# A tuned attention and feed-forward kernel whose written order is planned anew: sixteen planning passes, loads assumed at their full listed time, the first value load moved to GpSimd's queue

## The chip, the cores and the metric

One core of a Trainium2 chip runs the whole program. TensorE (PE) multiplies, and its weight loads are shown as PEld; VectorE (DVE), ScalarE (ACT) and GpSimd (POOL) work between the products; SyncE (SP) issues nearly all transfers. The metric is the device time of one execution in microseconds (us), smaller is better.

## The reference, cut to what matters

```python
def _attn_ref(q, k, v):                      # (4, 12, 448, 64) each
    scores = scale * np.matmul(q, k.transpose(0, 1, 3, 2)) - np.log(S)
    attn = 1.0 / (1.0 + np.exp(-scores))     # sigmoid, no sum over a row
    return np.matmul(attn, v)
def _moe_ref(x, w1, w2, w3, w_out):          # x: (1792, 768)
    h = np.maximum(np.maximum(x @ w1, x @ w2), x @ w3)
    return h @ w_out
def _moe2_ref(x, w_gate, w_val, w_out):      # d_ff 1536
    g = x @ w_gate
    return (g / (1.0 + np.exp(-g)) * (x @ w_val)) @ w_out
```

The output of attention, its heads side by side, goes through `_moe_ref` and the result through `_moe2_ref`. Everything is float32.

## The kernel before, in words

Every float32 factor of a dense product is split into a high and a low part, and three products of parts make one of the whole. The 1792 tokens are worked in two sets: set 0 holds the first 768 tokens, set 1 the other 1024.

**Stages on TensorE.** Attention runs in 12 quads (a quad is two pairs of heads of one batch), each of seven score groups: three of the first pair (`ps<-qq,kk`, six matmuls each), one that serves both (`ps<-qT,kT`), three of the second. ScalarE turns each group into `a` by one sigmoid (`a<-ps`), and later matmuls multiply `a` with the values (`av<-a,rv`). Two `ps` buffers exist, so that score group n+2 needs the sigmoid of group n. Once the first batches are through, products of the first dense layer of set 0 (`m<-x,w`, 18 matmuls each, 36 such products) stand between the groups. Then come the second layer of set 0, both layers of set 1 (by a scheme of seven products in place of eight), the gated layer for both sets (factors named `T` for set 1, `Z` for set 0) and the output product.

**Loads.** A pair needs four transfers each for `rq` and `rk` (56 KB each) and a quad three for `rv`. VectorE transposes `rq` and `rk` to `qT` and `kT`, and ScalarE, VectorE or GpSimd split these into `qq` and `kk`. A dense weight comes as `wraw` (768 KB, two buffers); ScalarE rewrites its words in two steps (`r<-wraw`, L483 and L496) and VectorE in two more (`c`), since the words must be put into the range of the parts; then it is split into `w`, and `c` is stored (`dp<-c`) for set 1.

**Who sets the order.** No engine chooses at run time. The program writes down tasks with their possible engines, an assumed duration and a due time; `Plan.order` runs through them once with a model of engines, queue and buffers, always starts the task that can start first (within a small slack the one with the earliest due time) and so fixes engine and place of every instruction. An instruction that waits holds everything behind it on its engine. A transfer on SP is assumed to take `SPF` = 0.88 of its listed time in a common queue, plus `TAIL` = 1800 ns, and SP's issue of one to take `ISSUE` = 530 ns. Due times come from TensorE's planned order and are passed back once over the tasks (`due_times`).

Of the kernel before, what the change touches and what calls it, by code (L numbers as in the profile page):

```python
# [1 line left out]

# [55 lines left out]
SPF = 0.88  # L58
# [12 lines left out]
NEAR = 6  # L71
AHEAD0 = 170.0 * 1000.0
# [6 lines left out]
ISSUE = 530.0  # L79
# [4 lines left out]
BACK = 3  # L84
# [7 lines left out]
class Plan:  # L92
# [9 lines left out]
    def __init__(self):  # L102
        self.tasks = []
        self.kind = None

    def add(self, opts, fn, reads=(), writes=(), after=(), due=math.inf, tail=0.0, port=False, wait=(), early=0.0, issues=1, late=0.0):
        deps = {id(w): w for w in (*after, *wait) if w is not None}
        deps.update((id(w), w) for b in (*reads, *writes) for w in b.writers)
        data = {id(w) for b in (*reads, *writes) for w in b.writers} | {id(w) for w in wait}
        new = [b.root for b in writes if b.root.ring is not None]  # L110
        deps.update((id(b.ring.opener), b.ring.opener) for b in new if b.ring.opener is not None)
        load = opts.get("sp", 0.0) * SPF
        if load:
            opts = {"sp": ISSUE * issues}
        t = Task(opts, fn, list(deps.values()), new, due, tail, port)
        t.data, t.early, t.load, t.late, t.issues = data, early, load, late, issues
        t.kind = self.kind
        for b in writes:
            b.writers.append(t)
        for b in (*reads, *writes):  # L120
            b.root.users.append(t)
        self.tasks.append(t)
        return t

    def due_times(self):
        for t in reversed(self.tasks):
            t.due = t.aim
            d = LEAD.get(t.kind, 0.0) + max(min(t.opts.values()), t.load)
            for s in t.succ:
                lat = (0.0 if "pe" in t.opts and "pe" in s.opts else self.LAT) + (t.tail if id(t) in s.data else 0.0)  # L130
                t.due = min(t.due, s.due - d - lat)

# [6 lines left out]
    def order(self):  # L139
# [40 lines left out]
        while open_:  # L180
# [13 lines left out]
            first = min(x[0] for x in best[e])  # L194
# [22 lines left out]

    def run(self, engines):
        for t in self.tasks:
            for d in t.deps:  # L220
                d.succ.append(t)
        self.due_times()
        length, done = self.order()
        for t, e, at in done:
# [4 lines left out]
        return length  # L229
# [27 lines left out]
def sigmoid_attention_max_ffn_silu_ffn(tc, q, k, v, w1, w2, w3, wo, wg, wv, wo2, out):  # L257
# [505 lines left out]
    def load_pair(b, h0):  # L763
# [15 lines left out]
        for src, r in ((q, rq), (k, rk)):  # L779
# [35 lines left out]
        fetch(rv, 2200.0, load_v, 3, "pairv" if b or h0 else "pair")  # L815
        return rq, rk, rv

    half_p = [slice(0, D), slice(D, P)]
# [531 lines left out]
    def gated(facs1, kept):  # L1350
# [5 lines left out]
        def factors(w, i):  # L1356
            plan.kind = "w"
            if i == 0:
                if id(w) in again:
                    left = left_again(again[id(w)])  # L1360
                    plan.kind = "b"
                    return left
                again[id(w)] = []
            left = seven(w, i, None if i else again[id(w)])
# [3 lines left out]
        ts = {}  # L1368
        for j, (w, use) in enumerate(((wg, silu(1, ts)), (wv, gate(1, ts, 0)))):
            left = factors(w, 0)  # L1370
            stream(1, left, facs[1], use)
            plan.kind = "x"
            facs[0].append(recall(j, kept[j]))
        rows, sums = EARLY_ROWS, 0
        for i in range(1, KG // 2):
            ts = {}
            for j, w in enumerate((wg, wv)):
                left = factors(w, i)
                for s in (1, 0):
                    stream(s, left, facs[s], gate(s, ts, i) if j else silu(s, ts))  # L1380
                    if len(facs[0]) < HD:
                        plan.kind = "x"
                        facs[0].append(recall(2, kept[2]))
                        plan.kind = "b"
                plan.kind = "w"
                if (i > 1 or j) and rows >= 2 * (sums + 1):
                    rows_sums(sums, due_p + 20000.0)
                    sums += 1
                if rows < KG:
                    rows_ahead(rows, due_p + 20000.0)  # L1390
                    rows += 1
                plan.kind = "b"
            if i == BACK:
                ts = {}
                for j, w in enumerate((wg, wv)):
                    stream(0, factors(w, 0), facs[0], gate(0, ts, 0) if j else silu(0, ts))
# [127 lines left out]

    plan.kind = "h"
    attention()
    turn([att, ps], [pmb, half, rest0])
    plan.kind = "w"
    for u in range(NU):
        weight(0, u)  # L1530
    todo = [(w, 2 * i + j) for i in range(KG // 2) for w in (wg, wv) for j in range(2)]
    for i, (w, f) in enumerate(todo[:NEAR]):
        ahead(w, f, False, AHEAD0 + (i + 1) * (AHEAD1 - AHEAD0) / NEAR, raw, AHEAD0 + i * (AHEAD1 - AHEAD0) / NEAR)
# [20 lines left out]
    for f in range(EARLY_ROWS):  # L1554
        rows_ahead(f, due_p)
    facs = second_layer(1, hs)
# [38 lines left out]
```

## Time and profile before

| what | value |
|---|---|
| median of 3 runs | 962.94 us (962.07 to 963.49) |
| profiled execution | 964.14 us, its span 962.0 us |
| instructions in the span | 13288 |
| TensorE busy | 942.6 us, 98% |
| VectorE, ScalarE, GpSimd busy | 667.5, 444.0, 92.1 us |
| mean granted TensorE clock | 0.990 |
| moved by DMA | 174.16 MB, 181 GB/s |

The span goes from the first to the last instruction; the execution's own time is 2.14 us longer. TensorE is nearly always busy, so time can change where it waits, where its clock is low, or where its work itself changes.

### The profile page before, as it was taken

What the parts mean: (1) busy time and instruction counts of PE and PEld (TensorE: products, weight loads), DVE (VectorE), ACT (ScalarE), POOL (GpSimd) and SP (SyncE); (2) the same over time, 40 slices, a digit from 0 to 9 for tenths busy, and PEclk for the clock granted to TensorE, in tenths of its full rate; (3) what the DMA queues carried; (4) which work ended last, traced back from release to release, by engine and by line L of the source; (5) the groups of instructions that cost most, each with busy time, mean ns of one, the idle gap of its engine ahead of it and who ended that gap; (6) DMA issues with size and microseconds to landing.
All of it is one profiled execution on the core that took longest, in us unless ns stands there. A gap on an engine that the chain in (4) does not pass through costs nothing.

```text
span 962.0 us, 13288 instructions
## 1 busy us (share of the span) xinstructions
PE 942.6 (98%) x4969; PEld 793.9 (83%) x4969; DVE 667.5 (69%) x1015; ACT 444.0 (46%) x620; POOL 92.1 (10%) x76
## 2 busy tenths in 40 slices
PE   8999989999999999999999999999999999999998
PEld 3444757877799888887888888888988989999998
DVE  5646565456568888998889965666456659998672
ACT  5657555466556545455665523233133325333330
POOL 0000000000010113221013201110010100000000
PEclk9998989999999999999999999999999999999999
DMA  7678878856569755556758474745844538621211
GB/s 115 130 142 191 222 197 213 243 187 203 189 194 324 238 187 180 179 172 197 256 187 278 148 224 140 225 164 171 282 141 138 169 106 326 230 83 50 99 58 66
DMA packets 196160, 174.16 MB, mean 181 GB/s; under 512 B 98304, under 2 KB 174592, under 8 KB 196096
## 3 DMA queue, kind: packets, MB, share of 16 engines
q1 hardware_dynamic: 192848, 172.91, 59.1%
q10 hardware_dynamic: 3248, 0.40, 0.3%
q8 instruction: 39, 0.64, 0.3%
q14 instruction: 25, 0.20, 0.1%
HBM read 115.74 MB, written 57.54 MB: 180 GB/s over the span
## 4 chain that ended last, share of the span: by engine, by line
PE 86%; DMA 5%; DVE 3%; SPq 2%; ACT 2%; issue 1%; DVEq 0%; ACTq 0%
PE m L1013 32%; PE av L1013 22%; PE mm L1013 22%; PE av L894 5%; PE ps L865 4%; DMA wraw<-in_moe_w_dram 2%; SPq L785 2%; DMA rk<-in_k_dram 1%; PE ps L858 1%; DMA rq<-in_q_dram 1%; DMA w<-dlS 1%; DVE S L622 1%; DMA dp<-S 1%; DVE Z L381 0%; DVE u L1193 0%
## 5 line engine op out<-in xcount | busy, mean ns | idle before, releaser
L1013 PE MATMUL mm<-T,w 128*128 128x512 f32 x567 | 138.0, 391 | 0.0
L1013 PEld LDWEIGHTS mm<-T,w 128*128 128x128 f32 x567 | 106.1, 188 | 21.6 <-DVE u L1193 0.4
L1013 PEld LDWEIGHTS m<-x,w 128*128 128x128 f32 x648 | 112.9, 190 | 11.4 <-issue 6.4
L1013 PE MATMUL m<-x,w 128*128 128x384 f32 x648 | 120.2, 341 | 0.0
L878 ACT ACTIVATE a<-ps,bias 128x896 f32<-128x896 f32 x84 | 80.8, 1003 | 42.9 <-PE ps L865 35.0
L1013 PE MATMUL m<-T,w 128*128 128x512 f32 x378 | 92.9, 390 | 0.0
L1013 PE MATMUL av<-T,w 128*128 128x512 f32 x378 | 92.5, 389 | 0.0
L1193 DVE TENSOR_TENSOR u<-mm,u 128x512 f32<-128x512 f32 (+1 forms) x93 | 59.0, 635 | 46.0 <-PE mm L1013 45.7
L1013 PEld LDWEIGHTS av<-T,w 128*128 128x128 f32 x378 | 71.0, 188 | 14.8
L1013 PEld LDWEIGHTS m<-T,w 128*128 128x128 f32 x378 | 70.8, 188 | 14.3
L865 PEld LDWEIGHTS ps<-qq,kk 64*128 64x128 f32 x432 | 45.9, 254 | 41.7 <-ACT a L878 28.6
L894 PE MATMUL av<-a,rv 128*64 128x448 f32 (+1 forms) x384 | 75.7, 564 | 0.1
L378 ACT CAST w<-G 128x768 fp32r<-128x768 f32 x47 | 39.4, 838 | 78.7 <-PE m L1013 33.7
L865 PE MATMUL ps<-qq,kk 64*128 64x448 f32 x432 | 62.6, 413 | 11.3 <-ACT a L878 10.2
L504 DVE SCALAR_TENSOR_TENSOR c<-c,r 128x768 int32<-128x768 int32 x48 | 51.1, 1064 | 31.9 <-ACT r L496 31.6
L483 ACT ACTIVATE r<-wraw 128x768 int32<-128x768 uint32 x48 | 43.7, 911 | 47.5 <-DMA wraw<-in_moe_w_dram 32.9
L1013 PE MATMUL mm<-Z,w 128*128 128x384 f32 x324 | 62.3, 336 | 0.0
L1013 PEld LDWEIGHTS mm<-Z,w 128*128 128x128 f32 x324 | 57.4, 188 | 1.9 <-DMA w<-dlS 0.2
L1013 PE MATMUL av<-wr,w 128*128 128x384 f32 x288 | 52.5, 334 | 0.0
L496 ACT ACTIVATE r<-wraw 128x768 f16<-128x768 f32 x48 | 52.0, 1084 | 0.5
L381 DVE TENSOR_TENSOR w<-G,w 128x768 fp32r<-128x768 f32 x49 | 46.6, 953 | 5.4 <-ACT w L378 5.4
L1013 PEld LDWEIGHTS av<-wr,w 128*128 128x128 f32 x288 | 50.1, 188 | 0.0
(141 smaller groups left out, 1482.7 us busy)
## 6 DMA issues: line engine op xcount, KB each, us to landing
cc<-dp SPq DMA_DIRECT2D x30, 768.0 KB, 5.1
dp<-c SPq DMA_DIRECT2D x48, 384.0 KB, 4.2
wraw<-in_moe_w_dram SPq DMA_DIRECT2D x18, 768.0 KB, 6.2
wraw<-in_moe_w_gate_dram SPq DMA_DIRECT2D x12, 768.0 KB, 4.9
wraw<-in_moe_w_val_dram SPq DMA_DIRECT2D x12, 768.0 KB, 5.1
cc<-in_moe_w_out_dram SPq DMA_DIRECT2D x12, 768.0 KB, 4.7
G<-dg SPq DMA_DIRECT2D x28, 320.0 KB, 7.0
rq<-in_q_dram SPq DMA_DIRECT2D x96, 56.0 KB, 2.6
```

The costliest lines, as they stand in the source:

```text
L378: (eng.copy if eng is nc.scalar else eng.tensor_copy)(o, i)
L381: eng.tensor_tensor(out=o, in0=a, in1=b, op=ALU.subtract)
L483: lambda e: e.activation(rb_at(), word(0).bitcast(U32), AF.Copy, scale=0.875 * 2.0 ** -29, bias=0.4999),
L496: lambda e: e.activation(rb_at().bitcast(F16).rearrange("p (c two) -> p c two", two=2)[:, :, 1], word(1).bitcast(F32), AF.Copy, scale=2.0 ...
L504: lambda e: e.scalar_tensor_tensor(c_at().bitcast(I32), c_at().bitcast(I32), 3, rb_at(), ALU.logical_shift_left, ALU.bitwise_or),
L622: return lambda e: e.tensor_tensor(out=o(), in0=x(), in1=y(), op=kind)
L785: eng.dma_start(out=r.t[D * j + 32 * e:D * j + 32 * e + 32], in_=src[b, h0 + j, :, 32 * e:32 * e + 32].rearrange("(c i) d -> i c d", i=32),)
L865: nc.tensor.matmul(psb.t[:, j, :S], kk.t[half_p[j], wh, cols], qq.t[half_p[j], xh], start=(i == 0), stop=(i == 2),)
L878: lambda e: e.activation(ab.t, psb.t[:, :, :S], AF.Sigmoid, bias=bias, scale=SCALE),
L894: nc.tensor.matmul(accs[g].t[half_p[j], :S], pairs[g][2].t[at, 2 * g + j, c], ab.t[at, j], start=first[g], stop=last[g],)
L1013: nc.tensor.matmul(acc.at(n), l(), r(), start=first and i == 0, stop=last and i == len(terms) - 1, skip_group_check=not (first and last),)
L1193: lambda e: e.tensor_tensor(out=o.t[:, :n], in0=acc.at(n), in1=x.t[:, :n], op=ALU.add),
```

## The change

Lines with `+` are new. The planner draws its plan sixteen times. After a pass, `again` takes the order that came out: due times of TensorE's tasks become the start times of a schedule without holes, tasks are ranked as placed, and a task that reuses a buffer hands its due time to the users of the buffer before it (`behind`). The pass with the smallest `cost` (holes in TensorE's planned order, plus `HALF` for each hole over 1600 ns) is kept; from the fourth pass on the due times of the best are shaken by up to 300 ns. On ScalarE and VectorE (`LOOK`) a task that is due sooner, and could start before the chosen one ends, goes first. Transfers are assumed to take 1.0 instead of 0.88 of their listed time up to the second layer of set 1 (`plan.full`), and 0.88 from there on; an issue 550 instead of 530 ns.

By hand, two loads move: the `rk` of the second pair, which ScalarE's queue issued, goes to SP's queue ahead of the same pair's `rq`, and the `rv` of the first quad goes from SP's queue to GpSimd's. The rewritten `gated` (not shown) puts down the same tasks as before with the values given: `BACK` was 3 already, so the first gated pair of set 0 stood in the middle of that stage before, too.

```diff
-SPF = 0.88
+SPF = 1.0
+SPF1 = 0.88
...
-ISSUE = 530.0
+ISSUE = 550.0
...
+LOOK = ("act", "dve")
+HALF = 2500.0
+TRIALS = 16
+SETTLE = 3
+SHAKE = 300.0
...
-        load = opts.get("sp", 0.0) * SPF
+        load = opts.get("sp", 0.0) * (SPF if self.full else SPF1)
...
-        for t in reversed(self.tasks):
+        for t in sorted(self.tasks, key=lambda t: t.rank, reverse=True):
...
+            for s in t.behind:
+                t.due = min(t.due, s.due - max(min(t.opts.values()), t.load) - (t.tail if "sp" in t.opts else 0.0) - self.LAT)
...
+            if e in LOOK:
+                soon = at + t.opts[e]
+                for x in best[e]:
+                    if at < x[0] < soon and x[1] < soon - SLACK and t.due > x[0] + x[2].opts[e] and x[1] < t.due:
+                        at, _, t = x
+                        soon = at
...
+    def cost(self, done):
+
+        last = total = 0.0
+        for at, t in sorted(((at, t) for t, e, at in done if e == "pe"), key=lambda x: x[0]):
+            total += max(0.0, at - last) + (HALF if at - last > 1600.0 else 0.0)
+            last = at + t.opts["pe"]
+        return total, last
...
+        for i in range(TRIALS):
+            if i >= SETTLE:
+                for t, state in best[3]:
+                    t.aim, t.rank, t.behind = state
+            self.due_times()
+            if i >= SETTLE:
+                for t in self.tasks:
+                    if "pe" not in t.opts:
+                        t.due += chance.uniform(-SHAKE, SHAKE)
+            length, done = self.order()
+            cost = self.cost(done)
+            if best is None or cost < best[0]:
+                self.again(done)
+                best = cost, length, done, [(t, (t.aim, t.rank, t.behind)) for t in self.tasks]
...
-            elif src is k and b == 0 and h0 == 2:
-                fetch_act(r, load, 4)
+            elif b == 0 and h0 == 2:
+                late_q.append((r, load))
             else:
                 fetch(r, 1700.0, load, 4, "pair")
+        if late_q:
+            for r, load in reversed(late_q):
+                fetch(r, 1700.0, load, 4, "pair")
+            late_q[:] = []
...
-        fetch(rv, 2200.0, load_v, 3, "pairv" if b or h0 else "pair")
+        if b or h0:
+            fetch(rv, 2200.0, load_v, 3, "pairv")
+        else:
+            plan.add({"pool": 3000.0}, lambda _: load_v(nc.gpsimd), writes=[rv], tail=TAIL + 1500.0)
...
+    plan.full = False
     facs = second_layer(1, hs)
```

The order of nearly every engine changes somewhere, but the counts do not: TensorE has the same 432 + 48 score matmuls, 192 of values and 4041 dense ones, VectorE 1021 instead of 1017 instructions, ScalarE (its transfers aside) 627 instead of 622, GpSimd 72 instead of 81. From the second layer of set 0 on, TensorE's own order is the same as before; only its order within attention and the first layer differs.

Three places follow, in the program's rows (line, operation, out<-in, shape, and how many in a row). First SP at the program's start; before:

```order
L785 DMA rq<-in_q_dram 32x14x32 x4
L785 DMA rk<-in_k_dram 32x14x32
L806 DMA rv<-in_v_dram 128x4x192
L810 DMA rv<-in_v_dram 64x2x64 x2
L785 DMA rq<-in_q_dram 32x14x32 x8
```

Now:

```order
L852 DMA rq<-in_q_dram 32x14x32 x4
L852 DMA rk<-in_k_dram 32x14x32 x5
L852 DMA rq<-in_q_dram 32x14x32 x8
L852 DMA rk<-in_k_dram 32x14x32 x4
L852 DMA rq<-in_q_dram 32x14x32 x4
```

The three `rv` transfers are gone from the place after the fifth transfer, and the second pair's four `rk` stand there; ScalarE issues three transfers at the start where it issued seven, and GpSimd issues the three of `rv` right after its memset.

Second, SP around the first dense weight (`wraw<-in_moe_w_dram`); before, where 108 transfers stand ahead of it:

```order
L785 DMA rk<-in_k_dram 32x14x32 x4
L785 DMA rq<-in_q_dram 32x14x32 x4
L468 DMA wraw<-in_moe_w_dram 128x6x256
L785 DMA rk<-in_k_dram 32x14x32 x4
L806 DMA rv<-in_v_dram 128x4x192
```

Now, where 71 transfers stand ahead of it:

```order
L877 DMA rv<-in_v_dram 128x4x192
L881 DMA rv<-in_v_dram 64x2x64 x2
L852 DMA rq<-in_q_dram 32x14x32 x4
L852 DMA rk<-in_k_dram 32x14x32 x4
L852 DMA rq<-in_q_dram 32x14x32 x4
L535 DMA wraw<-in_moe_w_dram 128x6x256
L877 DMA rv<-in_v_dram 128x4x192
```

The load stands 37 transfers nearer to the start, and 12 sigmoids earlier on ScalarE: its first `r<-wraw` followed the 35th sigmoid and now follows the 23rd.

Third, TensorE from the 22nd score group on, which is what these sigmoids wait for and release; before:

```order
L865 MATMUL ps<-qq,kk 128x448 x12
L894 MATMUL av<-a,rv 64x448 x4
L865 MATMUL ps<-qq,kk 128x448 x6
L858 MATMUL ps<-qT,kT 64x448 x4
L894 MATMUL av<-a,rv 64x448 x4
L865 MATMUL ps<-qq,kk 128x448 x12
```

Now:

```order
L940 MATMUL ps<-qq,kk 128x448 x12
L969 MATMUL av<-a,rv 64x448 x4
L940 MATMUL ps<-qq,kk 128x448 x6
L933 MATMUL ps<-qT,kT 64x448 x4
L940 MATMUL ps<-qq,kk 128x448 x6
L969 MATMUL av<-a,rv 64x448 x4
```

The first row holds groups 22 and 23, the third group 24, the fourth group 25. Group 26 stood behind four value matmuls and now stands directly behind group 25.

## Rows read from the trace of the kernel before

**Rows 1.** The page: busy time of the engines.

```profile
PE 942.6 (98%) x4969; PEld 793.9 (83%) x4969; DVE 667.5 (69%) x1015; ACT 444.0 (46%) x620; POOL 92.1 (10%) x76
```

**Rows 2.** Stretches: PE, PEld, DVE, ACT, POOL busy us, PEclk, DMA share, GB/s.

```profile
60.00:80.00 20.00, 17.02 (x96) 6.67 (x90) 11.61 (x24) 10.02 (x13) 1.14 (x1) 0.83 0.74 149
...
140.00:282.00 142.00, 142.00 (x834) 112.52 (x834) 80.07 (x128) 79.13 (x98) 7.07 (x6) 1.00 0.72 216
282.00:560.00 278.00, 275.44 (x1276) 235.07 (x1275) 239.03 (x346) 155.19 (x235) 50.43 (x37) 1.00 0.63 207
```

**Rows 3.** PE in order of time: start, duration, tiles [idle before <-releaser].

```profile
7.78 1.88 PE L865 MATMUL ps<-qq,kk 64*128 64x448 f32 x12 [1.06 <-ACT kk L378]
11.82 1.49 PE L865 MATMUL ps<-qq,kk 64*128 64x448 f32 x6 [2.16 <-ACT a L878]
13.24 1.77 PE L858 MATMUL ps<-qT,kT 64*64 64x448 f32 x8
...
47.65 0.95 PE L865 MATMUL ps<-qq,kk 64*128 64x448 f32 x6
48.53 0.98 PE L858 MATMUL ps<-qT,kT 64*64 64x448 f32 x8
49.44 1.72 PE L894 MATMUL av<-a,rv 128*64 128x448 f32 x8
...
73.65 1.49 PE L865 MATMUL ps<-qq,kk 64*128 64x448 f32 x6 [2.98 <-ACT a L878]
75.07 3.25 PE L894 MATMUL av<-a,rv 128*64 128x448 f32 x8
...
118.52 3.40 PE L1013 MATMUL m<-x,w 128*128 128x384 f32 x18
...
130.16 1.49 PE L865 MATMUL ps<-qq,kk 64*128 64x448 f32 x6 [4.81 <-ACT a L878]
131.59 4.81 PE L1013 MATMUL m<-x,w 128*128 128x384 f32 x18
```

**Rows 4.** PE's waits by releaser: us in total, times, longest.

```profile
PE ps L865 <- ACT a L878: 10.2, 4, 4.8
PE m L1013 <- DVE Z L381: 1.9, 2, 1.3
```

**Rows 5.** ACT in order of time.

```profile
10.29 0.56 ACT L378 CAST kk<-kT 128x448 fp32r<-128x448 f32 x1 [2.57 <-DVE kT L834]
...
48.70 1.97 ACT L878 ACTIVATE a<-ps,bias 128x896 f32<-128x896 f32 x2 [1.25 <-PE ps L865]
...
71.47 0.91 ACT L483 ACTIVATE r<-wraw 128x768 int32<-128x768 uint32 x1 [4.36 <-DMA wraw<-in_moe_w_dram]
```

**Rows 6.** The chain of work that ended last: start, duration, what.

```profile
65.35 6.09 DMA wraw<-in_moe_w_dram
...
120.14 8.10 DMA wraw<-in_moe_w_dram
```

**Rows 7.** SP's issues in order of time: start, duration, tiles, count.

```profile
2.73 0.48 SPq L785 DMA_DIRECT2D rk<-in_k_dram  x1
3.26 0.48 SPq L806 DMA_DIRECT2D rv<-in_v_dram  x1
...
6.17 5.53 SPq L785 DMA_DIRECT2D rq<-in_q_dram  x8
...
43.25 1.99 SPq L785 DMA_DIRECT2D rk<-in_k_dram  x4
```

**Rows 8.** DVE in order of time, at the start.

```profile
5.47 0.65 DVE L834 STREAM_TRANSPOSE qT<-rq 128x448 f32<-128x448 f32 x1 [4.61 <-DMA rq<-in_q_dram]
...
9.62 0.65 DVE L834 STREAM_TRANSPOSE kT<-rk 128x448 f32<-128x448 f32 x1 [1.17 <-DMA rk<-in_k_dram]
```

**Rows 9.** DMA issues: count, KB each, median us from issue to landing.

```profile
rk<-in_k_dram SPq DMA_DIRECT2D x89, 56.0 KB, 2.5
rv<-in_v_dram SPq DMA_DIRECT2D x12, 384.0 KB, 4.1
```

More of the change, by code (lines that the diff above doesn't have):

```diff
@@ L71 @@
 NEAR = 6
+FIRST = 0
+FIRST0 = 12000.0
+FIRST1 = 12000.0
 AHEAD0 = 170.0 * 1000.0
@@ L104, in __init__ @@
         self.kind = None
+        self.full = True
     def add(self, opts, fn, reads=(), writes=(), after=(), due=math.inf, tail=0.0, port=False, wait=(), early=0.0, issues=1, late=0.0):
@@ L216, in order, with again @@
         return max(t.end for t in self.tasks), done
+    def cost(self, done):
[4 more added lines that the diff above has]
+        return total, last
+    def again(self, done):
+        rings = {}
+        for i, (t, e, at) in enumerate(done):
+            t.behind, t.place = [], i
+            for b in t.new:
+                rings[id(b.ring)] = b.ring
+        for i, (t, e, at) in enumerate(sorted(done, key=lambda x: (x[2], x[0].place))):
+            t.rank = i
+        for r in rings.values():
+            for b, c in zip(r.order, r.order[r.bufs:]):
+                t = min((u for u in c.users if any(x is c for x in u.new)), key=lambda u: u.rank)
+                for u in b.users:
+                    if u.rank < t.rank:
+                        u.behind.append(t)
+        last = None
+        for at, t in sorted(((at, t) for t, e, at in done if e == "pe"), key=lambda x: x[0]):
+            last = at if last is None else last
+            t.aim = last
+            last += t.opts["pe"]
     def run(self, engines):
-        for t in self.tasks:
+        for i, t in enumerate(self.tasks):
             for d in t.deps:
                 d.succ.append(t)
-        self.due_times()
-        length, done = self.order()
-        for t, e, at in done:
+            t.rank, t.behind = i, []
+        best, chance = None, random.Random(1)
+        for i in range(TRIALS):
[12 more added lines that the diff above has]
+                best = cost, length, done, [(t, (t.aim, t.rank, t.behind)) for t in self.tasks]
+            elif i < SETTLE:
+                self.again(done)
+        for t, e, at in best[2]:
             for b in t.new:
@@ L1357, in factors, with fetch @@
             plan.kind = "w"
[L1358 to L1364, printed above, removed]
+            if (id(w), i) in again:
+                left = left_again(again[id(w), i])
+            else:
+                if i < KEPT:
+                    again[id(w), i] = []
+                left = seven(w, i, again.get((id(w), i)))
             plan.kind = "b"
             return left
[L1368 to L1371, printed above, removed]
+        def fetch():
             plan.kind = "x"
-            facs[0].append(recall(j, kept[j]))
+            facs[0].append(recall(len(facs[0]), kept[len(facs[0])]))
+            plan.kind = "b"
         rows, sums = EARLY_ROWS, 0
-        for i in range(1, KG // 2):
+        for i in range(KG // 2):
             ts = {}
@@ L1523, in output @@
                         send(s, c, 0, 1, u[k, 1])
+    todo = [(w, 2 * i + j) for i in range(KG // 2) for w in (wg, wv) for j in range(2)]
     plan.kind = "h"
@@ L1528, in sigmoid_attention_max_ffn_silu_ffn @@
     plan.kind = "w"
+    for i, (w, f) in enumerate(todo[:FIRST]):
+        ahead(w, f, False, FIRST0 + (i + 2) * FIRST1, raw, FIRST0 + i * FIRST1)
+    for i, (w, f) in enumerate(todo[FIRST:NEAR]):
+        n = NEAR - FIRST
+        ahead(w, f, False, AHEAD0 + (i + 1) * (AHEAD1 - AHEAD0) / n, raw, AHEAD0 + i * (AHEAD1 - AHEAD0) / n)
     for u in range(NU):
         weight(0, u)
-    todo = [(w, 2 * i + j) for i in range(KG // 2) for w in (wg, wv) for j in range(2)]
-    for i, (w, f) in enumerate(todo[:NEAR]):
-        ahead(w, f, False, AHEAD0 + (i + 1) * (AHEAD1 - AHEAD0) / NEAR, raw, AHEAD0 + i * (AHEAD1 - AHEAD0) / NEAR)
     plan.kind = "b"
```

32 lines of the change are left out of this document (18 added, 14 removed).

## The prediction

> **What bounds the kernel now.** I read the page first, then the stretches, then TensorE's order of time, and at each hole the engine that ended it. The page says that TensorE is busy for 942.6 of 962.0 us [rows 1], so the work itself cannot shrink by an order, and an upper limit for this change is the time that TensorE waits or runs slowly. The stretches show where that is: from 140 us on TensorE is busy throughout up to 282 us and for 275.44 of 278 us behind that, at a granted clock of 1.00, while the stretch around 70 us has 17.02 of 20 us and a clock of 0.83 [rows 2]. So nearly all that can be won lies in attention, before 140 us.
>
> TensorE's order of time gives the places [rows 3]. After its first two score groups it waits 2.16 us at 11.82, then 2.98 us at 73.65 and 4.81 us at 130.16. All three end with a sigmoid, and with a fourth small one they make the 10.2 us that TensorE waits for `a` [rows 4]. Behind each the matmuls run at about half their rate: six score matmuls take 1.49 us where they take 0.95 at full rate, the group that serves both pairs 1.77 against 0.98, eight value matmuls 3.25 against 1.72, a product of the first layer 4.81 against 3.40 [rows 3]. That is the 1.2 GHz level of the clock; the reader should take each wait and its slow tail as one loss:
> - start: 2.16 + (1.49 - 0.95) + (1.77 - 0.98) = 3.5 us;
> - 70 us: 2.98 + 0.54 + (3.25 - 1.72) + 0.79, where I take the fourth term from the same kind of group at the start, = 5.8 us;
> - 125 us: 4.81 + 0.54 + (4.81 - 3.40) = 6.8 us.
>
> Together 16.1 us. A wait of 1.06 us (the row at 7.78) was followed by twelve matmuls in 1.88 us, far from half rate, and the waits of up to 1.3 us for `Z` [rows 4] lie in a stretch with clock 1.00 [rows 2]; so the slow tail came after waits of 2.16 us and more, and not after those of 1.3 and less.
>
> What ends these sigmoids is not TensorE. At the start the sigmoid stands on ScalarE behind a cast of `kk` that waited for VectorE until 10.29 [rows 5], and VectorE waited for `rk` of the second pair until 9.62 [rows 8]. At 70 us ScalarE had stood 4.36 us on `r<-wraw` at 71.47 [rows 5], for a weight issued at 65.35 that took 6.09 us to land; at 128 us another one, issued at 120.14, took 8.10 [rows 6]. The sigmoids behind were free to run.
>
> **The change, part by part.** The planning itself runs before the program exists and costs nothing on the chip. Counts of instructions stay within a few, and TensorE's are equal, so the sum is made of waits.
>
> *Start.* `rk` of the second pair now follows the fifth transfer on SP. That one was issued at 2.73 and took 0.48 us [rows 7]; four more at that pace (1.99 us for four, row at 43.25) end at 5.3, and 2.5 us to land [rows 9] make 7.8. VectorE is then still in its first four operations, which begin at 5.47 and hold it at 0.65 each, with small waits, to about 8.5 [rows 8]. The second `kT` starts at 8.5 instead of 9.62, the cast on ScalarE 1.1 us before 10.29, and score group 3, which followed that cast by 1.53 us, at 10.7 instead of 11.82. The wait shrinks from 2.16 to 1.04 us, as long as the one that had no slow tail, so 0.54 + 0.79 go too: 2.5 us won. The bounds are 0 and the whole 3.5. SP lost time at the start next to ScalarE's seven issues: three `rv` from 3.26 to 6.17 and eight `rq` in 5.53 us where four take some 2.08 with their gaps [rows 7]. If four `rk` meet the same, `kT` comes as late as before.
>
> *`rv` of the first quad by GpSimd.* No transfer of GpSimd is in this trace. The values are first needed behind groups 3, 4 and 5, at 10.7 + 0.88 + 0.91 + 0.88 = 13.4 us. By SP they take 4.1 us to land [rows 9]; issued among GpSimd's first instructions, they have some 12 us. I put this at nothing, hidden under the score groups; the lower bound is nothing as well, the upper one is a rival below. Nothing is queued behind these issues that early: the low part of the second pair's `kk`, which was GpSimd's next work, is VectorE's now.
>
> *The first weight.* This is the one new wait that I see. The load is SP's 72nd transfer. Before, the 71st began at 43.25 [rows 7], the 72nd thus at 43.75. At the undisturbed pace of 0.52 per transfer the 72nd would start at 2.73 + 67 x 0.52 = 37.6; both are bounds. The first eleven transfers behind the fifth took 8.4 us (2.91 + 5.53) where the pace gives 5.7, and that was next to ScalarE's issues; I take 2.3 of the 2.7 back and put the load at 41.4. Landing takes between 4.1 us (half as large a load, [rows 9]) and 8.10; I take the 6.1 of the same load at the end of attention-only traffic [rows 6]: 47.5. ScalarE's first rewrite stands directly ahead of the 24th sigmoid. It takes 0.91 us and the sigmoid 1.0 [rows 5], so the latter ends at 49.4. Score group 26 needs the buffer which that sigmoid frees. Group 24 was at 47.65 and is 2.5 us earlier now, 45.15; group 25 follows 0.88 and group 26 another 0.91 later, at 46.95, because the value matmuls that stood between have moved behind it. The wait is 49.45 - 46.95 = 2.5 us. From the bounds it is nothing (load at 37.6, landed at 41.7) or 6.9 us (43.75 + 8.1). With 2.5 us it is of the kind that had a slow tail; tails cost 1.3, 2.9 and 2.0 us at the three places, I take 1.9. Loss: 4.4 us. What was won at the start is lost here: SP's queue does not know that TensorE is early.
>
> *The two old places.* Behind this point the order gives the loads more room. The second weight's rewrite stands behind sigmoid 28, and its load is the 84th transfer, twelve places behind the first: 41.4 + 12 transfers (three of them `rv`) is about 48.5, landed by 54.6, while sigmoid 28 ends near 56.4: four groups behind 49.4, each 0.88 us and half of the 1.72 of eight value matmuls [rows 3]. The same count leaves the third weight 3 us to spare and the fourth 8. Rewrites six to eight, of which the seventh caused the wait at 130 us, now stand between sigmoids 44 and 47, where TensorE has eight products of the first layer in a row, 144 matmuls or 25 us, for which no sigmoid is needed. So I count both losses as gone: 5.8 + 6.8 = 12.6 us. Transfers have room for it: the DMA share is 0.72 on the mean from 140 to 282 us, where the same weights were loaded [rows 2]. The upper bound of what comes back is the rival on repeated waits.
>
> *Behind attention.* TensorE's order is the same from the second layer of set 0 on, and planned loads are again at 0.88. VectorE is busy 239.03 of 278 us there [rows 2], and the waits for `Z` of 1.9 us [rows 4] have a different neighbour now (some of `Z` stands ahead of sums that free a bank). I leave these 1.9 us as they are; bounds are none of it and twice of it.
>
> **Sum.** 2.5 + 12.6 - 4.4 = 10.7 us. From the profiled execution, 964.14, that is 953.4; the median shown is 1.2 below that execution, so 952.2 us. Its own range, with the start between 1.5 and 3.5 and the first weight's loss between 3 and 6, is 949.5 to 955.
>
> **A rule that speaks against it.** VectorE has nothing to do until 5.47 us, when its first load lands [rows 8]. The Trainium skill, DMA: Bandwidth & Descriptors, section SWDGE vs HWDGE vs iDMA, says that a transfer issued by GpSimd has its descriptors written by software into SBUF, and that VectorE in its two-port fast modes locks GpSimd out of it, which transfers of SP and ScalarE do not suffer. By that rule the values are safe if GpSimd is through by then and could be late if it is not; no run here shows it yet.
>
> **Rivals.**
> - *The first weight is in time.* If SP keeps its bare pace the load lands before ScalarE comes to it. For it: in [rows 7] four transfers take 1.99 us wherever nothing disturbs; against it: by 43.25 the pace of before had lost 6 us to such disturbances, most of them not at the start. Then 15.1 us are won: 964.14 - 15.1 - 1.2 = 947.8.
> - *One more wait of the old kind.* The second or third rewrite meets its load late, or a due-time swap on VectorE delays a transpose. For it: weights took up to 8.10 us to land [rows 6], and 2 us of room do not cover that. One wait with tail is worth 5.8 or 6.8 us: 958 to 959.
> - *The plan does not do what it says.* The losses only move, since the order comes out of assumed times as before, and TensorE waits as long in all: with the start's 2.5 us or without, 961 to 963. For it: 0.88 to 1.0 adds 0.4 us to a weight that took 6.1 to 8.1. Against it: the new order has most rewrites where TensorE needs no sigmoid.
> - *First values late, slower.* If GpSimd's transfer lands after 13.4 us, TensorE stands in line at its first value matmuls, with every later score group behind them, 1 us for 1 us. It decides from 24.1 us on, when all 10.7 are gone; landing at 28 us, the time would be 952.2 + 14.6 = 966.8. For it: nothing in the trace bounds such a transfer from above; against it: 12 us are three times what the same transfer takes by SP.
>
> **How the numbers follow.** 0.46 for the forecast, 0.20 for the weight in time, 0.16 for one more wait, 0.10 for losses that only move, 0.08 for slower (late values, or several new waits at once). A measurement of this kernel can tell about 0.2%, or 1.9 us, from no change. Faster is the first three, 0.82; same 0.10; slower 0.08. The range reaches from the weight in time with the whole start and `Z` won as well (947.8 - 1.0 - 1.3 = 945.5) to the border of the losses that only move, 961.0; what is left out is about 0.18.
>
> **What would show it.** In the changed profile: group 3 at about 10.7 us with no slow tail; value matmuls at 13.4 with no transfer named as releaser; the first `wraw` issued near 41.4, and a wait of about 2.5 us of TensorE for a sigmoid near 47 us with a clock at half level behind it; no wait above 1.5 us from there to 282 us; the first layer over by about 271 us instead of 282; `Z` waits as before. The prediction is wrong if rows on ScalarE show `r<-wraw` ahead of a late sigmoid again between 60 and 140 us, or if the wait at the start does not shrink.

## The result, and the profile after

The changed kernel takes 950.80 us (median of four runs, 949.83 to 952.54), beside 963.22 us (962.07 to 964.54) for the kernel before: a ratio of 0.9873 [0.9853, 0.9892]. Predicted were 952.2 us, with 949.5 to 955 as the forecast's own range. The profiled execution took 950.76 us, 13.4 less than the one of before; its span is 13.0 less. One execution of a later kernel ("other shakes" below) took 2657.56 us and is left out of that kernel's numbers.

The page of the changed kernel, its first lines and the granted clock in the 40 slices:

```profile
span 949.0 us, 13281 instructions
PE 936.5 (99%) x4969; PEld 792.4 (84%) x4969; DVE 668.0 (70%) x1019; ACT 444.9 (47%) x625; POOL 86.0 (9%) x70
PEclk9999999999999999999999999999999999999999
```

Against [rows 1], TensorE is busy for 6.1 us less while it does the same products: what went is slow time, and 6.9 us of waiting. Where, the stretches show (columns: stretch, length, then busy time and instructions of TensorE, weight loads, VectorE, ScalarE, GpSimd; granted clock, DMA share, GB/s):

```profile
0.00:20.00 20.00, 14.53 (x72) 7.03 (x72) 10.33 (x20) 9.01 (x12) 2.84 (x8) 0.91 0.75 120
60.00:80.00 20.00, 19.07 (x124) 10.88 (x124) 12.83 (x24) 14.36 (x19) 1.83 (x1) 1.00 0.87 224
120.00:140.00 20.00, 20.00 (x114) 13.85 (x114) 12.50 (x21) 10.05 (x13) 2.31 (x2) 1.00 0.92 227
282.00:560.00 278.00, 277.32 (x1280) 236.40 (x1279) 240.52 (x353) 160.63 (x243) 50.49 (x36) 1.00 0.64 218
```

Around 70 us TensorE now has 19.07 of 20 us at a full clock, where [rows 2] has 17.02 at 0.83, and around 130 us it never stops. From 282 us on it waits 0.68 instead of 2.56 us. What is still waited for, in TensorE's waits (total, times, longest, in us):

```profile
PE ps L940 <- ACT kk L445: 3.8, 1, 3.8
PE ps L940 <- ACT a L953: 2.4, 5, 1.1
...
PE av L1088 <- DMA w<-dlS: 0.7, 2, 0.4
```

Sigmoids cost 2.4 us where they cost 10.2, and the `Z` of [rows 4] are gone from the list. The one long wait is new: 3.8 us for `kk`, at the very start. TensorE's order of time has it in its first row, and the second place of interest, the first weight, in its last three rows:

```profile
10.04 2.50 PE L940 MATMUL ps<-qq,kk 64*128 64x448 f32 x12 [3.76 <-ACT kk L445]
12.76 1.49 PE L940 MATMUL ps<-qq,kk 64*128 64x448 f32 x6 [0.22 <-ACT a L953]
...
16.23 1.72 PE L969 MATMUL av<-a,rv 128*64 128x448 f32 x8
...
48.17 0.98 PE L933 MATMUL ps<-qT,kT 64*64 64x448 f32 x8
50.22 0.95 PE L940 MATMUL ps<-qq,kk 64*128 64x448 f32 x6 [1.06 <-ACT a L953]
51.10 1.72 PE L969 MATMUL av<-a,rv 128*64 128x448 f32 x8
```

The first score groups begin at 10.04 instead of 7.78 and the first value matmuls at 16.23 instead of 15.86 [rows 3]. The start lost 0.4 us where 2.5 were to be won, and it still has its slow tail: six score matmuls in 1.49 us at 12.76. At the first weight TensorE waits 1.06 us, and the matmuls behind it run at full rate.

Why the start is late is seen in the chain of work that ended last (start, duration, what):

```profile
3.98 4.25 DMA rk<-in_k_dram
8.23 0.64 DVE qT L909
```

VectorE's first transpose begins at 8.23, behind a 56 KB piece of `rk` that took 4.25 us to land. Before, VectorE began at 5.47 [rows 8]. The transfers of the first 8 us name what lay beside it (for a queue: packets, MB, and their share of the time of the 16 DMA engines; for a group of transfers: their number, the size of one, median us from issue to landing):

```profile
q1 hardware_dynamic: 4061, 0.50, 56.1%
q0 software_dynamic: 176, 0.46, 17.7%
...
rk<-in_k_dram SPq DMA_DIRECT2D x5, 56.0 KB, 5.0
...
rv<-in_v_dram POOLq DMA_DIRECT2D x2, 32.0 KB, 5.5
```

GpSimd's three transfers (q0) have landed by about 8.5 us, long before they are needed. But they moved 0.46 MB in 176 packets beside SP's 4061 small ones (q1, 0.50 MB), and SP's five `rk` took 5.0 us at the median.

### The profile page after: what moved, and what is told of

The parts are those of the page before. It is cut to its first block, busy times and chain, and to the rows that moved or that the text cites. A ratio compares the mean times of both kernels' runs of the same rounds, so it can differ in the third digit from the quotient of the medians.

```text
span 949.0 us, 13281 instructions
## 1 busy us (share of the span) xinstructions
PE 936.5 (99%) x4969; PEld 792.4 (84%) x4969; DVE 668.0 (70%) x1019; ACT 444.9 (47%) x625; POOL 86.0 (9%) x70
## 4 chain that ended last, share of the span: by engine, by line
PE 94%; DMA 3%; ACT 1%; DVE 0%; SPq 0%; issue 0%; DVEq 0%; ACTq 0%
PE m L1088 35%; PE mm L1088 24%; PE av L1088 23%; PE av L969 7%; PE ps L940 5%; DMA w<-dlS 1%; PE ps L933 1%; DMA rk<-in_k_dram 1%; ACT a L953 1%; DMA wraw<-in_moe_w_dram 1%; SPq L852 0%; DMA rq<-in_q_dram 0%; DVE qT L909 0%; DVE qq L448 0%; DVE kT L909 0%
## 5 line engine op out<-in xcount | busy, mean ns | idle before, releaser
L1088 PEld LDWEIGHTS m<-x,w 128*128 128x128 f32 x648 | 111.5, 188 | 10.2 <-issue 4.6
L1268 DVE TENSOR_TENSOR u<-mm,u 128x512 f32<-128x512 f32 (+1 forms) x93 | 59.2, 637 | 50.4 <-PE mm L1088 50.2
L571 DVE SCALAR_TENSOR_TENSOR c<-c,r 128x768 int32<-128x768 int32 x48 | 48.0, 999 | 42.7 <-ACT r L563 42.5
L445 ACT CAST w<-G 128x768 fp32r<-128x768 f32 x44 | 36.8, 838 | 78.8 <-PE m L1088 29.9
L969 PE MATMUL av<-a,rv 128*64 128x448 f32 (+1 forms) x384 | 73.2, 554 | 0.0
L445 ACT COPY u<-av 128x512 f32<-128x512 f32 (+1 forms) x32 | 17.5, 546 | 81.4 <-PE av L1088 76.6
```

The source lines that it names most:

```text
L445: (eng.copy if eng is nc.scalar else eng.tensor_copy)(o, i)
L571: lambda e: e.scalar_tensor_tensor(c_at().bitcast(I32), c_at().bitcast(I32), 3, rb_at(), ALU.logical_shift_left, ALU.bitwise_or),
L969: nc.tensor.matmul(accs[g].t[half_p[j], :S], pairs[g][2].t[at, 2 * g + j, c], ab.t[at, j], start=first[g], stop=last[g],)
L1088: nc.tensor.matmul(acc.at(n), l(), r(), start=first and i == 0, stop=last and i == len(terms) - 1, skip_group_check=not (first and last),)
L1268: lambda e: e.tensor_tensor(out=o.t[:, :n], in0=acc.at(n), in1=x.t[:, :n], op=ALU.add),
```

## The experiments

The theory with which I began: the gain is that no late weight stands ahead of a sigmoid any more; the **passes** do it, since only they know TensorE's planned times, and the start is lost to **contention**, because `rv` from GpSimd shares the DMA engines with the first `rq` and `rk`. The rivals: the assumed **rate** of 1.0 alone does it; and the start is late because SP now issues five `rk` in a row (**queue**).

In all plans TensorE's order is the same from the second layer of set 0 on, so each kernel's span can be cut at that layer's first matmul. *Front* is what lies ahead of it, *behind* the rest of the span; both are in us and from the profiled executions. Each ratio is to runs of the kernel before on the same chip, with its 95% interval; medians from different chips are not to be compared. "Other shakes" draws other random shifts of the due times, and "no look" is without the look-ahead on ScalarE and VectorE. Two small differences are in every kernel with the new planner and are not taken apart: the issue time of 550 ns, and that the tasks of six gated weights (`todo[:NEAR]`) are now put down ahead of the first layer's. The kernel before with the rate alone has neither.

| kernel | rate, passes | median | ratio to before | front | behind |
|---|---|---|---|---|---|
| before | 0.88, 1 | 963.22 | 1 | 281.4 | 680.6 |
| after | 1.0, 16 | 950.80 | 0.9873 [0.9853, 0.9892] | 270.8 | 678.2 |
| after, a second time | 1.0, 16 | 950.78 | 0.9880 [0.9854, 0.9906] | 270.7 | 679.4 |
| hand moves undone | 1.0, 16 | 949.90 | 0.9875 [0.9848, 0.9901] | 269.4 | 677.8 |
| `rv` held back | 1.0, 16 | 949.63 | 0.9875 [0.9854, 0.9897] | 268.6 | 678.7 |
| the same, planned | 1.0, 16 | 951.09 | 0.9887 [0.9869, 0.9905] | 270.5 | 677.7 |
| `rv` on SP, later | 1.0, 16 | 954.93 | 0.9926 [0.9905, 0.9947] | 271.6 | 682.0 |
| other shakes | 1.0, 16 | 950.54 | 0.9882 [0.9856, 0.9907] | 270.9 | 680.3 |
| 48 passes, `rv` held, planned | 1.0, 48 | 952.46 | 0.9901 [0.9880, 0.9922] | 271.6 | 679.3 |
| no look | 1.0, 16 | 954.97 | 0.9931 [0.9911, 0.9950] | 270.3 | 681.7 |
| three passes | 1.0, 3 | 958.03 | 0.9961 [0.9945, 0.9976] | 270.5 | 685.2 |
| low rate | 0.88, 16 | 957.39 | 0.9958 [0.9945, 0.9970] | 268.9 | 685.0 |
| one pass | 1.0, 1 | 964.45 | 1.0034 [1.0015, 1.0053] | 271.2 | 690.9 |
| before, with the rate | 1.0, 1 | 959.99 | 0.9985 [0.9970, 0.9999] | 271.3 | 686.5 |

**The first values held back.** Everything stays in the order of the changed kernel, but GpSimd copies eight columns of the first `kT` into `rv` ahead of its transfers, which write over them; so they start only once the first pair has landed.

```diff
+        def held_v(_):
+            for kt in first_kt:
+                nc.gpsimd.tensor_copy(rv.t[:, 0, 0, :8], kt.t[:, :8])
+            load_v(nc.gpsimd)
...
-            plan.add({"pool": 3000.0}, lambda _: load_v(nc.gpsimd), writes=[rv], tail=TAIL + 1500.0)
+            plan.early_v = plan.add({"pool": 3000.0}, held_v, writes=[rv], tail=TAIL + 1500.0)
```

> The changed kernel with one thing different: GpSimd issues the first quad's rv only after the first kT is written (a copy of eight columns of kT into rv's place, overwritten by the load, stands ahead of it); every other row of the plan is the same. Theory, contention: the rv packets filled the 16 DMA engines between 3.5 and 6.5 us and held up the first pair's rq and rk. Then the third rq lands near 4.7 us as before the change instead of 6.47, the first score group starts near 7.8 instead of 10.04, the tenth transfer of SP is issued before 5.5 instead of at 6.49, and the time falls by 1 to 2.5 us against the changed kernel (948.3 to 949.8), less than the 2.2 us of the start if the wait for the first weight near 49 us grows. Rival, the start is late for another cause (five rk in a row on SP, or VectorE's order): the first score group stays within 0.5 us of 10.04 and the time within 0.5 us of the changed kernel's.

Transfers of the first 8 us, then TensorE's order of time:

```profile
rk<-in_k_dram SPq DMA_DIRECT2D x5, 56.0 KB, 3.1
```

```profile
7.87 1.83 PE L951 MATMUL ps<-qq,kk 64*128 64x448 f32 x12 [0.36 <-ACT kk L447]
10.60 0.94 PE L951 MATMUL ps<-qq,kk 64*128 64x448 f32 x6 [0.90 <-ACT a L964]
...
13.52 1.72 PE L980 MATMUL av<-a,rv 128*64 128x448 f32 x8
...
48.04 0.94 PE L951 MATMUL ps<-qq,kk 64*128 64x448 f32 x6 [1.59 <-ACT a L964]
```

With SP's five `rk` in the same places, they land in 3.1 instead of 5.0 us, the third group stands at 10.60 and the value matmuls at 13.52: within 0.15 us of what the prediction had worked out for a start that `rv` does not touch. So contention is the cause and the queue is not. Eleven profiles here have five `rk` in a row on SP: they take 4.8 to 5.5 us at the median in the seven where GpSimd issues `rv` at once, and 2.6 to 3.1 in the four where `rv` is held or comes later. The value matmuls begin 2.7 us earlier; the first weight's wait takes 0.5 us of that back (1.59 for 1.06), so the front is 2.2 us shorter, and the span 1.7. The time does not show it (0.9875 against 0.9873): 1.7 us is near what a comparison can tell. A wait for `w` from memory behind the border is 1.3 us here, but it is 0.7 and 2.0 us in two profiles of the changed kernel itself.

**One pass.** Rate, issue time, look-ahead and hand moves stay.

```diff
-TRIALS = 16
+TRIALS = 1
```

> The changed kernel with TRIALS = 1: no pass is fed back, loads still at the full listed time, look-ahead and both moved loads kept. The first dense weight is then SP's 113th transfer and stands behind sigmoid 37, near where it was before the change (109th, 35). Theory, the passes: what was won is the earlier place of the weights, so both old waits of TensorE (some 3 to 5 us with slow tails, between 60 and 140 us) are back in some form and the time is 956 to 963. Rival, the assumed rate: planned with slower loads the weights are not waited for even at their old places; then no wait above 2 us stands between 60 and 140 us and the time is 949 to 953.

Stretches:

```profile
60.00:140.00 80.00, 80.00 (x487) 53.21 (x486) 47.41 (x83) 51.82 (x68) 9.45 (x7) 1.00 0.83 205
282.00:560.00 278.00, 270.18 (x1223) 228.23 (x1223) 235.42 (x351) 148.25 (x224) 48.18 (x36) 0.99 0.62 208
```

My theory fell here: without any feedback both old places are gone, 80.00 of 80 us at a clock of 1.00. The rival fares no better: it had 949 to 953 us. The time is that of the kernel before, even 0.34% more, for behind 282 us TensorE loses 7.8 us to waits, and a slow tail at the 1.2 GHz level of the clock follows one of them. The largest of these waits is that for `w`, and the order of time of TensorE, ScalarE and VectorE, a few rows of each, says why:

```profile
305.88 0.98 PE L1088 MATMUL av<-h,w 128*128 128x384 f32 x2 [3.28 <-DVE w L445]
307.13 5.31 PE L1088 MATMUL av<-h,w 128*128 128x384 f32 x16 [0.27 <-DVE w L448]
...
302.64 0.48 ACT L445 COPY t<-mm 128x384 f32<-128x384 f32 x1 [4.95 <-PE mm L1088]
303.02 1.06 ACT L563 ACTIVATE r<-wraw 128x768 f16<-128x768 f32 x1
...
304.11 0.96 DVE L571 SCALAR_TENSOR_TENSOR c<-c,r 128x768 int32<-128x768 int32 x1 [4.66 <-ACT r L563]
305.18 0.56 DVE L445 CAST w<-c 128x768 fp32r<-128x768 f32 x1
```

The second rewrite of a weight was written down behind a copy `t<-mm`, for which ScalarE waited 4.95 us until TensorE had made `mm`; then VectorE waited 4.66 us for the rewrite, and TensorE 3.28 us for `w`, with a slow tail behind (two and sixteen matmuls in 0.98 and 5.31 us, where eighteen of the first layer take 3.40 [rows 3]: 2.9 us more). What was late here was no transfer but a place in ScalarE's order.

**The kernel before with the rate alone.** Its own planner, one pass, no look-ahead, loads as they were; TensorE's order is the old one row for row. It turns the last experiment round: the rate without the rest of the change.

```diff
-SPF = 0.88
+SPF = 1.0
+SPF1 = 0.88
...
+    plan.full = False
     facs = second_layer(1, hs)
```

> The kernel before with the assumed rate alone: SPF = 1.0 up to the second layer of set 1, one pass, everything else as before. TensorE's order is row for row that of before; the first weight is SP's 109th transfer behind sigmoid 35, as before. Theory, the passes: the waits near 70 and 125 us stay, perhaps shorter by a microsecond each, time 958 to 964. Rival, the assumed rate: both waits shrink below 1.5 us, time 950 to 954.

The waits of TensorE:

```profile
PE ps L867 <- ACT a L880: 3.8, 4, 2.2
PE av L1015 <- DVE w L380: 2.8, 1, 2.8
```

The rate of 1.0 alone shortens the front by 10.1 us, as the whole change does (10.6). And it too gives 5.9 us back behind it, with a wait at the same place, 2.77 us at 305.44 for a `w` of VectorE (the 2.2 us for a sigmoid are those of the old start). 0.15% are left. The rival was right on the two waits, and its 950 to 954 us missed.

**Sixteen passes at the low rate.** All else is as in the changed kernel.

```diff
-SPF = 1.0
+SPF = 0.88
```

> The changed kernel with SPF = 0.88 throughout: sixteen passes, loads assumed as fast as before the change. The first weight is SP's 72nd transfer and stands behind sigmoid 23 as in the changed kernel. Theory, the passes: no wait above 2 us between 60 and 140 us, time 949 to 954. Rival, the assumed rate: waits for sigmoids behind late weights are back between 40 and 140 us, 4 us or more in all, time 956 to 962.

```profile
PE m L1088 <- DVE Z L448: 4.3, 1, 4.3
```

The front is 268.9, among the shortest: feedback and look-ahead without the rate remove the two old places as well. So neither is needed for the front, and either is enough. They do it in different ways, which ScalarE's waits for a weight at its first rewrite show, from 30 to 140 us (in total, times), in this order: before, rate alone, passes at the low rate, changed kernel:

```profile
ACT r L483: 18.9, 6
ACT r L485: 3.3, 2
ACT r L550: 19.7, 8
ACT r L550: 6.4, 4
```

Planned with slower loads, the rewrites hardly wait any more. With the passes at the low rate ScalarE stands as long as before, yet TensorE waits only 0.3 us in all for sigmoids: the long waits (3.25 us up to 99.0, 3.88 up to 118.4, 5.87 up to 130.5) now end beside first-layer products, up to 108 matmuls in a row, which need no sigmoid. The changed kernel has some of both.

Behind the border, one wait of 4.25 us for `Z` at 531.32 and its slow tail, about 2.4 us (two matmuls in 1.01 us, then nine of `mm<-T,w` in 3.99, which take 2.20 in the run with one pass at full clock), cover the 6.8 us by which that part is longer than in the changed kernel. So the time missed the 949 to 954 us that the theory gave.

**Hand moves undone**, in the sixteen passes: `rk` goes back to ScalarE's queue and `rv` to SP's; and beside it, on the same chip, **the changed kernel once more**.

```diff
-            elif b == 0 and h0 == 2:
-                late_q.append((r, load))
+            elif src is k and b == 0 and h0 == 2:
+                fetch_act(r, load, 4)
...
-        if b or h0:
-            fetch(rv, 2200.0, load_v, 3, "pairv")
-        else:
-            plan.add({"pool": 3000.0}, lambda _: load_v(nc.gpsimd), writes=[rv], tail=TAIL + 1500.0)
+        fetch(rv, 2200.0, load_v, 3, "pairv" if b or h0 else "pair")
```

> The changed kernel with both hand-moved loads put back (second pair's rk by ScalarE's queue, first rv by SP's), planned anew in sixteen passes. Theory, the hand moves cancel each other: the first score group is back near 7.8 us, group 3 near 11.8 with a slow tail, the first value matmuls near 15.9, and the time is within 2 us of the changed kernel's. Rival, they pay: first value matmuls later than 16.2 and the time more than 2 us longer. Rival, they cost: more than 2 us shorter.

> The changed kernel itself, unaltered, beside the other kernels of this call, so that they are compared with it on the same chip. Both theories expect its ratio to the kernel before inside 0.9853 to 0.9892 again, and first values landed near 8.5 us with the first score group near 10.

TensorE's order of time at the start, with the moves undone:

```profile
7.50 1.66 PE L937 MATMUL ps<-qq,kk 64*128 64x448 f32 x12
11.49 0.94 PE L937 MATMUL ps<-qq,kk 64*128 64x448 f32 x6 [2.33 <-ACT a L950]
...
14.41 1.72 PE L966 MATMUL av<-a,rv 128*64 128x448 f32 x8
```

949.90 beside 950.78 us: the two moves by hand are worth nothing that can be measured. The old wait of the start is there (2.33 us), but this time with no slow tail behind it. The changed kernel's second profile tells how far one kernel differs from itself: its first score groups begin at 9.49 and its value matmuls at 16.74, where the first profile has 10.04 and 16.23, and the part behind the border is 1.2 us longer.

**The first values on SP, later.** With `rk` on SP and `rv` behind the second pair's first transfers, the start has neither ScalarE's queue nor GpSimd's packets.

```diff
-            plan.add({"pool": 3000.0}, lambda _: load_v(nc.gpsimd), writes=[rv], tail=TAIL + 1500.0)
+            late_v.append((rv, load_v))
...
+            fetch(*[(v_, 2200.0, lv) for v_, lv in late_v][0], 3, "pair")
```

> The changed kernel with the first quad's rv back on SP, but behind the second pair's rk and rq (17 transfers ahead of it... 13 of them of the first two pairs), planned anew; the second pair's rk stays on SP. Theory, contention of the large rv packets with the first pair's loads: with rv behind them the first score group is near 7.8 us, group 3 near 10.7 with no slow tail, the first value matmuls near 13.5, all better than both hand versions (16.2 and 14.4); the first layer ends near 268.5. The time is within 2 us of 949.5, since what the start wins is waited for at the first weight. Rival, GpSimd's queue helps: the values then land after 13.4 and TensorE waits for them, first value matmuls later than 15.

```profile
10.19 0.94 PE L941 MATMUL ps<-qq,kk 64*128 64x448 f32 x6 [0.91 <-ACT a L954]
...
13.11 1.72 PE L970 MATMUL av<-a,rv 128*64 128x448 f32 x8
...
48.44 0.98 PE L934 MATMUL ps<-qT,kT 64*64 64x448 f32 x8 [1.76 <-ACT a L954]
49.35 2.81 PE L970 MATMUL av<-a,rv 128*64 128x448 f32 x8
```

This is the best start of all, 3.1 us ahead of the changed kernel at the value matmuls, and its front of 271.6 us is as long as any plan's. A later quad's `rv` costs 0.6 us at 37.6, and the first weight 1.76 us with a slow tail (eight value matmuls in 2.81 us). So what is won at the start is lost again, much of it at the first weight, as the prediction's step has it: 0.7 us more of wait and 1.1 of tail. About 1.5 us of the loss up to the border are not traced to one place. Behind it, another wait of 1.8 us for `u` of VectorE follows at 544 us, with a slow tail too, and 954.93 us misses the 949.5, give or take 2, that was expected.

**The held load, known to the planner**: the copy's `kT` stands in the task as `reads`, so that the passes can plan with it; and **48 passes** on the same program.

```diff
+                plan.add({"pool": 3000.0}, held_v, reads=[t], writes=[v_], tail=TAIL + 1500.0)
```

> The changed kernel with GpSimd's rv held until the first kT, as in the earlier run, but known to the planner, which draws anew. Theory: the start is as in that run (first score group near 7.9, first value matmuls near 13.5) and the time 947 to 951; the plan's luck behind 400 us decides within that. Rival, the start counts in full: 946 to 948 whatever the rest.

> The planned hold of GpSimd's rv with 48 passes in place of 16: more draws to choose from. Theory, holes that the plan itself can see are what the draws remove: no wait above 1.5 us behind 282 us; time 946 to 950. Rival, more draws only fit the plan to its assumed times: the time is not below that of the same kernel with 16 passes, and a wait of 2 us or more appears somewhere.

In order of time, TensorE and GpSimd at the start (of the sixteen passes):

```profile
10.88 3.34 PE L948 MATMUL ps<-qq,kk 64*128 64x448 f32 x14 [2.57 <-POOL kk L448]
...
8.39 1.20 POOL L881 DMA_DIRECT2D rv<-in_v_dram  x2
9.68 1.15 POOL L448 TENSOR_TENSOR kk<-kT,kk 128x448 fp32r<-128x448 f32 x1
```

The planner gave GpSimd the low part of a `kk`. It stands behind the issues of the held transfers, which end at 9.6, and TensorE waits 2.57 us for it, with half rate behind. Neither this nor 48 passes beat the changed kernel. With 48 passes no wait behind 282 us is above 0.7 us, as the theory said, but the time, 952.46 us, is not in its 946 to 950.

**Which part of the planner keeps the rest.** Three kernels, each with one of these edits: no look-ahead, no choice among shaken plans, and other shakes.

```diff
-LOOK = ("act", "dve")
+LOOK = ()
...
-TRIALS = 16
+TRIALS = 3
...
-        best, chance = None, random.Random(1)
+        best, chance = None, random.Random(2)
```

> The changed kernel with LOOK = (): the look-ahead on ScalarE and VectorE off, sixteen passes and slower assumed loads kept. Theory, feedback of passes is what removes the waits of 2 to 3 us near 305 us and 497 to 504 us that stand in the one-pass plans: they stay away and the time is within 3 us of the changed kernel's. Rival, the look-ahead removes them: a wait above 2 us of TensorE for a late w stands between 300 and 310 us and the time is 4 us or more longer.

> The changed kernel with TRIALS = 3: three passes fed back one after the other, no shaken due times, so nothing is chosen among random variants. Theory, feedback: one or two fed-back passes are enough, no wait above 1.5 us between 290 and 320 us, time within 3 us of the changed kernel's. Rival, the choice among shaken plans: waits of 2 us and more remain behind 280 us and the time is 4 us or more longer.

> The changed kernel with another seed of the random shakes and nothing else changed: sixteen passes, another plan kept. Theory, the feedback and the assumed rate do the work up to 282 us and the kept plan only decides over single waits behind: end of the first layer at 269 to 272 as in all plans so far, no wait above 2 us before it, and the time 949 to 959, with a wait of 4 to 5 us for Z near 530 us if the draw is a bad one. Rival, the measured gain is the luck of one draw: waits of 3 us and more are back between 60 and 282 us and the time is above 959.

All three have the short front, and none has the wait at 305 us. Three passes lose 7 us behind the border, at one place (TensorE, then VectorE, in order of time):

```profile
533.51 1.01 PE L1088 MATMUL m<-Z,w 128*128 128x384 f32 x2 [4.85 <-DVE Z L448]
...
531.49 1.02 DVE L783 TENSOR_TENSOR tt<-tt,Z 128x384 f32<-128x384 f32 x1 [1.41 <-DMA tt<-dh]
...
532.91 0.55 DVE L448 TENSOR_TENSOR Z<-Z 128x384 fp32r<-128x384 f32 x1
```

VectorE stands behind a load of `dh`, and `Z` behind VectorE; a slow tail of some 2.3 us follows (nine matmuls of `mm<-T,w` in 3.83 us). This is also where the low rate lost 4.25 us. So the theory was right that two passes fed back keep the wait at 305 us away, and wrong that the time stays within 3 us of the changed kernel's. Without the look-ahead the kernel is 4 us longer, as the rival had it, but not by the rival's cause: the wait at 305 us did not return. One wait shows 1.8 us of the 4, for `u` at 542.93. Other shakes give 950.54 us (three executions, 950.18 to 953.00), as the changed kernel does, so its time does not hang on this one draw.

## Why the prediction was right

The time was right, its likeliest case happened, and the two terms that carried it did too; but three smaller terms were off, and that they nearly cancelled (2.9 us against it; 3.3 and 1.9 for it) is luck.

- **The two old places, 12.6 us: right.** No wait above 0.74 us from 60 to 140 us, the clock at 1.00, and TensorE is through with the first layer at 270.8 us, where about 271 was forecast. The reason in the text, that the new order gives rewrites room, holds: ScalarE's waits for weights fall from 18.9 to 6.4 us between 30 and 140 us. What gives them room was not settled there: the one rate constant is enough, and so are the passes without it, which leave the waits of ScalarE (19.7 us) and put them where TensorE needs no sigmoid.
- **The start, +2.5 us: wrong, -0.4.** The step that failed is "`rv` of the first quad by GpSimd. I put this at nothing". I asked whether the values themselves come late, and they don't: they landed by about 8.5 us for use at 16.2. The cost lay with the neighbours. With `rv` held back, SP's `rk` land in 3.1 us, not 5.0, and the forecast places (10.7 and 13.4) are met at 10.60 and 13.52; so the steps for `rk` were right, and the term was lost to contention. The Trainium skill, DMA: Bandwidth & Descriptors, section Issuing engines are not separate DMA queues, says that transfers of GpSimd, ScalarE and SP run on the same 16 DMA engines and interleave. The traces agree, 5.0 against 3.1 us, and this was the rule to weigh, rather than the one on VectorE's fast modes: VectorE had nothing to do until 8.2 us, so that one had no occasion to show itself here.
- **The first weight, -4.4 us: right mechanism, size off, -1.1.** The wait stands where it was put, ended by the sigmoid behind `r<-wraw`, at 49.2 to 50.2 instead of 47 to 49.5. The load was issued at 43.37, near the late bound of 43.75 and not at 41.4; it landed in 4.95 us, where 6.1 were taken; and TensorE itself was ready at 49.16, not 46.95, since its start had not been won. Where it had been won, the wait was 1.59 (`rv` held) and 1.76 us with a tail (`rv` on SP).
- **`Z`, no change: off by 1.9 us in our favour.** Those waits are gone. They are as much the draw's as the change's: three passes and the low rate have 4.9 and 4.3 us there, the other plans of sixteen passes at rate 1.0 none.

In all -0.4 - 1.1 + 12.6 + 1.9, less 0.7 us for a wait at 78.6, makes 12.3 of the 13.0 us by which the span shrank, where the sum had 10.7: 10.4 of the 10.6 us of the front, and 1.9 of the 2.4 behind it.

Of the rivals, "the losses only move" is what happens to this kernel with one pass (964.45), at places that the text had not looked at, behind attention. The step "TensorE's order is the same from the second layer on" was true, and said nothing of ScalarE and VectorE, whose places behind 282 us decide 13 us between the plans (677.7 to 690.9). That sixteen passes keep the gain there is shown. The wait at 305 us stands in both plans of one pass at the rate of 1.0, with the look-ahead and without, and in no plan of three or more; one pass and three differ by nothing else, so feeding passes back takes it away, as far as single plans can tell. What the other 13 passes and the look-ahead avoid further behind (7 and 4 us) is seen at single waits only and stays open.

## What to carry to other kernels

A load that is moved to an idle queue still shares the transfers of the others: ask not only when it lands but what lands beside it, and hold a load that has time until the urgent ones are through (here that won 2.7 us at the start, and nothing that the whole time shows). An engine's wait that is taken away early is worth only what the next late transfer leaves of it. When a plan changes by one constant, measure the front and what lies behind it apart: here every plan won 10 to 13 us ahead of one border, and up to 10 us of it came back behind.

## What the runs showed beyond that

The same wait was followed by the low clock in one run and not in another. TensorE's order of time, first with `rv` on SP, then without the look-ahead:

```profile
544.31 2.87 PE L1089 MATMUL mm<-Z,w 128*128 128x384 f32 x9 [1.80 <-DVE u L1269]
```

```profile
542.93 1.83 PE L1088 MATMUL mm<-Z,w 128*128 128x384 f32 x9 [1.80 <-DVE u L1268]
```

Both wait 1.80 us for `u` ahead of the same nine matmuls, which then take 2.87 us here and 1.83 there; and the 2.33 us at the start with the hand moves undone had no slow tail. So the border that the prediction read from the kernel before, between 1.3 and 2.16 us, is none; what decides is open.

SP's issue of the five `rk`, too, took longer with `rv` beside them. SP's order of time, in the changed kernel (4.06 us) and with `rv` held (2.64 us):

```profile
2.75 4.06 SPq L852 DMA_DIRECT2D rk<-in_k_dram  x5
```

```profile
2.74 2.64 SPq L854 DMA_DIRECT2D rk<-in_k_dram  x5
```
